# Third batch's first DFT moved off the first block's buffers and banks, with ScalarE's work for that block in another order

## The chip, the cores and the metric

The kernel runs on one core of a Trainium2 chip. Its time is the device time of one execution in microseconds (us); lower is better. The core has five instruction queues: TensorE (PE in the profile; PEld is its weight load), VectorE (DVE), ScalarE (ACT), GpSimd (POOL) and SyncE (SP, which here only issues transfers). Each queue runs its instructions in the order in which they stand.

## What is computed

```python
def reference(x, filt_r, filt_i, w_gate, w_noise, noise, w1, w2):
    # x (8, 2496, 256): Fourier filter along the sequence of each batch
    X = np.fft.rfft(x, axis=1)
    y = np.fft.irfft(X * (filt_r + 1j * filt_i)[None], n=2496, axis=1)
    # 19968 tokens of 256 features, 8 experts of width 1024, two experts a token
    t = y.reshape(19968, 256)
    logits = t @ w_gate + np.log1p(np.exp(t @ w_noise)) * noise
    top2, top2_w = two_best_and_their_softmax(logits)
    out = 0
    for e in range(8):
        for k in range(2):
            mask = top2[:, k] == e
            out[mask] += top2_w[mask, k, None] * (np.maximum(t[mask] @ w1[e], 0) @ w2[e])
    return out
```

All values are float32. The products of the expert part are made of three products of rounded halves each (`_mm3`: high by high, high by low, low by high).

## The kernel before

The work has two streams. The first filters one batch after the other by a transform of 39 x 64 points, works out the gate, and writes which token goes to which expert into a list. The second, the mixture of experts, takes the tokens of one expert in blocks of 512 from that list: it gathers their rows, multiplies with `w1`, applies relu, multiplies with `w2`, and adds the rows to the output. Batches 0 and 1 are filtered before the first block (the *early* part); the other batches are filtered beside the blocks.

The steps of the filter that matter here, with the lines of the profile and the names of their tiles:

- `s1`, the first DFT of a batch: 11 products of two groups (L319, bank `q1`). Each needs one load `x` (L305). ScalarE copies the result to a tile `c` (`c1`, L362), and SP writes it to a table `fd` in DRAM (L363), from which later steps read (`fx`, L370). In the early part the third batch (batch 2, products 22 to 32) has this step run too, two products in each time slot from slot 26.
- `t3` and `i2`, the inverse transform of a half batch `n` (n = 2 and 3 are the two halves of batch 1): six times a transposition (L494), a copy by ScalarE to `tf` (L499), a product (L516, bank `q6`), and a copy by ScalarE to `yt` (L526; for odd n also L529), which SP writes to `y` (L531). Transposition and product take turns on two banks, so a product waits until ScalarE has copied the one before it.
- the gate of a batch: products `lg` (L475 to L477), then a chain of small steps. ScalarE takes an exponential (L733), loads a table (`ACT_TABLE_LOAD`) and takes a logarithm (L736); VectorE works down to the counts `rs` (L737 to L772), with a second exponential by ScalarE (L766) between. TensorE makes prefix sums `rk` (L788 to L790), VectorE turns them into positions and `new` (L798 to L854), TensorE makes `sl` (L859, L860), VectorE makes `sval` (L861 to L880), TensorE makes `st` (L884), and VectorE makes the table `tab`. Then the list is built: 11 groups of products `ra` of masks `oc` (L921 to L926), a transposition (L933), and a scatter by GpSimd to `lst` (L945).
- `zero_out` writes zeros to the output rows of a batch in four parts (L293, 702 KB, the last 468 KB).

The steps of a block: SP reads its list (`lt`, L963), GpSimd gathers four tiles of rows (L999), ScalarE reorders them (L1049, `x32`), TensorE transposes (`xps`, L1057), ScalarE and VectorE split them into `mxh` and `mxl` (L1060, L1061). `w1` and `w2` come in four parts each through four slots of the tile `stage` and are split by ScalarE and VectorE (`wsplit`, L1107, L1108; w1 as `w1h` and `w1l`, w2 as `w`). Then eight times 6 products into a bank `hps` (L123 to L125), relu by ScalarE (L1150, `hh`) and the rest by VectorE (L1151, `hl`), and four times 24 products into `yps`. The first two blocks have rows of batch 0.

Three things set the order. `fft_stream` writes the early steps into numbered slots (`plan`), and `pin` ties each such instruction to the one pinned before it on its engine. Within that, a scheduler places instructions by its own estimate of times. And tiles of one tag share a few buffers in turn (`bufs`): the next user of a buffer waits for the last reader of the one before. PSUM banks go the same way, by tables:

```python
EARLY = {"q1": "hps", "q2": "hps", "q5": "yps", "q6": "yps", "u1": "xps"}
BANKS = {"hps": 2, "yps": 2, "xps": 1, "fps": 3}
MOVES = {..., 14: {"q3": "yps", "q4": "yps", "q5": "hps", "q6": "hps"}, 26: {"q4": "fps", "q5": "yps", "q6": "yps"}}
def ps(self, nm):
    tag = self.banks.get(nm, "fps") if self.early else "fps"
```

So a name that no table holds (`lg`, `rk`, `sl`, `st`, `ra`) takes one of the three banks `fps`, in the order in which the code asks. In slot 26 the code asks for `lg`, then for the third batch's products 22 and 23, then for `rk`, `sl` and `st` (all within slot 26, in `gating_more`), then in slot 27 for products 24 and 25. In the kernel before, the third batch's products take the two banks `hps`, its `x` the eight buffers `hh` and its `c` the eight buffers `hl`: the buffers and banks that the first block's eight results need.

Of the kernel before, what the change touches and what calls it, by code (L numbers as in the profile page):

```python
# [10 lines left out]
F32 = mybir.dt.float32  # L11
# [3 lines left out]
U16 = mybir.dt.uint16  # L15
AF = mybir.ActivationFunctionType
# [123 lines left out]

MOVES = {0: {"q3": "yps"}, 12: {"q3": "fps"}, 14: {"q3": "yps", "q4": "yps", "q5": "hps", "q6": "hps"}, 26: {"q4": "fps", "q5": "yps", "q6": "yps"}}


class Moe:
# [156 lines left out]
    def s1l(self, bt, g0):  # L301

        x = self.P.tile([128, 512], F32, name="x", **((dict(tag="w1l", bufs=4) if bt == 0 and g0 >= 16 else dict(tag="hh", bufs=8)) if self.early else dict(bufs=2)))

        self.lastx = self.nc.sync.dma_start(x, self.io["x"][bt, :, g0 * D:(g0 + 2) * D])  # L305
        x = x[:RP]
        self.xx[bt, g0] = x
        return self.lastx
# [50 lines left out]
    def s1e(self, bt, g0, q):  # L359
        nc, P, early = self.nc, self.P, self.early  # L360
        c = P.tile([120, 2, D], F32, name="c1", **(dict(tag="hl", bufs=8) if early else dict(bufs=1)))
        nc.scalar.copy(c, q.rearrange("p (g d) -> p g d", g=2))  # L362
        self.lastx = nc.sync.dma_start(self.Fd[bt][3 * g0:3 * g0 + 6].rearrange("(g q) k d -> (q k) g d", g=2), c)  # L363
# [144 lines left out]
    def i2(self, n, g0):  # L508
        nc, P, h = self.nc, self.P, n % 2
        Dh, Dl = self.cD  # L510
        th, tl = self.t3t.pop((n, g0))
        k = min(4, NG - g0)
        m = 128 * k
        p = self.ps("q6")
        if tl is None:
            nc.tensor.matmul(p[:RP, :m], self.rD, th[:120, :m], start=True, stop=True)  # L516
        else:
            nc.tensor.matmul(p[:RP, :m], Dh, th[:120, :m], start=True, stop=False)  # L518
            nc.tensor.matmul(p[:RP, :m], Dh, tl[:120, :m], start=False, stop=False)  # L519
            nc.tensor.matmul(p[:RP, :m], Dl, th[:120, :m], start=False, stop=True)  # L520
        w = 128 + E * h
        if n == 0:
            yt = P.tile([RP, 4, 128], F32, name="yt", tag=("mxl0", "mxh1", "mxl1")[g0 // 4 % 3], bufs=1)
        else:
            yt = P.tile([RP, 4, 128 + E], F32, name="yt", bufs=2)
        nc.scalar.copy(yt.bitcast(U16)[:, :k, :256].rearrange("p g (two d) -> p g two d", two=2),  # L526
                       p.bitcast(U16)[:RP, :2 * m].rearrange("p (g d two) -> p g two d", g=k, two=2))
        if h:
            nc.scalar.copy(yt[:, :k, 128:], self.dense[:, g0:g0 + k])  # L529
        y = self.y[BLK + n // 2 * ROWS:BLK + (n // 2 + 1) * ROWS].rearrange("(p g) d -> p g d", p=RP)  # L530
        nc.sync.dma_start(y[:, g0:g0 + k, h * 128:h * 128 + w], yt.bitcast(I32)[:, :k, :w])  # L531

    def fft_stream(self):
# [5 lines left out]
        N = 2 * NB  # L539
        self.fx, self.Fd = {}, {}  # L540
        todo = [(bt, g) for bt in range(NB) for g in range(0, NG, 2)]
# [10 lines left out]
        def s1(j):  # L552
            if self.early:
                self.s1(*todo[j])
                ahead(min(j + 9, 11 * (j // 11) + 11))
            else:
                ahead(j + 2)
                self.s1(*todo[j])
# [44 lines left out]
        at(8, self.setup2)  # L603
        at(20, ahead, 30)

# [17 lines left out]
        for i in range(4):  # L623
            at(18 + i, self.zero_out, 0, i)
            at(24 + i, self.zero_out, 1, i)

# [345 lines left out]
    def front(self, ent, fill=None):  # L972
# [6 lines left out]
        w1st = self.load_w(re, "w1", nt)  # L979
        w1 = [self.wsplit(w1st[q], "w1", q) for q in range(4)]  # L980
        w2st = self.load_w(re, "w2", nt)
# [51 lines left out]
    def turn(self, ent):  # L1033
# [8 lines left out]
        for kc in range(2):  # L1042
# [5 lines left out]
            else:  # L1048
                nc.scalar.copy(xu.rearrange("p (t d two) -> p t d two", t=nt, two=2),  # L1049
                               self.picked(ent).bitcast(U16)[:, :, 256 * kc:256 * kc + 256].rearrange("p t (two d) -> p t d two", two=2))  # L1050
            q.append(x)
        for kc in range(2):
            x = q[kc]
# [65 lines left out]
    def expert(self, parts, may, fill=None):  # L1119

        nc, P = self.nc, self.P
        self.parts, self.ahead, self.standing, self.early_l = parts, [], False, None
        self.fetch(lambda: True)
        cur = None
        while self.ahead:
# [10 lines left out]
            if not self.ahead or self.ahead[0][3] or sum(len(a[2][0]) for a in self.ahead) < 4:  # L1136
                self.fetch(may)
            third = ("xps", 1) if self.by_dma(ent) else ("yps", 2)
            hh = []
            for f in range(8):  # L1140
# [8 lines left out]
                l = P.tile([128, 512], R32, name="hl", bufs=8)[:, :w]  # L1149
                nc.scalar.activation(h, p, AF.Relu)  # L1150
                v = nc.vector.scalar_tensor_tensor(l, p, 0.0, f32v(h), op0=ALU.max, op1=ALU.subtract)  # L1151
                if f == 4:
                    self.early_l = v
                hh.append((h, l))
                if f % 2 and i == 0:
                    w2.append(self.wsplit(w2st[f // 2], "w2", f // 2))
                yield
            late = not self.ahead
            if late:
# [142 lines left out]
```

## Time and profile before

| | |
|---|---|
| time, three executions | 2263.53 us median, 2259.55 to 2263.73 |
| the profiled execution | 2255.39 us, span of its instructions 2253.5 us |
| TensorE busy | 2199.0 us (98% of the span), mean granted clock 0.992 |
| VectorE, ScalarE, GpSimd busy | 1621.7, 1240.4 and 955.1 us |
| first product of the first block | 166.11 us after the start |

A row of a timeline reads: start, duration, engine, line, operation, out<-in, shapes, count, and in brackets the idle time of the engine ahead of it and what ended it. Rows of equal instructions that follow each other are merged. A row of a window table gives, for each engine, the busy time within that stretch, then the granted TensorE clock (1.00 is full), the busy share of the DMA engines, and GB/s.

### The profile page before, as it was taken

Reading aid. Unit: us, or ns where it says so; the run is one execution under the profiler, and the core shown is the slowest. Engines: PE = TensorE matmul, PEld = TensorE weight load, DVE = VectorE, ACT = ScalarE, POOL = GpSimd, SP = SyncE. Lnnn points to the kernel's source line nnn. Section 1 sums busy time; section 2 is a strip of 40 time slices with the busy share of each in tenths; the row PEclk is TensorE's granted clock in tenths of the full one; section 3 lists DMA queues with packets and bytes.
Section 4 is the critical chain, followed back from the end, with each engine's and each line's share of the span. In section 5 each row is a group of like instructions: output and inputs, shape, how many; then the busy total and the mean of one; then the engine's idle time right before and its main releaser. Section 6 shows DMA issues by size and latency. Waiting matters only on the chain.

```text
span 2253.5 us, 39355 instructions
## 1 busy us (share of the span) xinstructions
PE 2199.0 (98%) x12599; PEld 1842.5 (82%) x12599; DVE 1621.7 (72%) x3494; ACT 1240.4 (55%) x2433; POOL 955.1 (42%) x822
## 2 busy tenths in 40 slices
PE   8779999999999999999999999999999999999998
PEld 5448888888888888888888888888888888889997
DVE  4858679779877987697668866795555555667886
ACT  6765655656566456445544455444444434557876
POOL 4013345335333444354344533355454544455442
PEclk9989999999999999999999999999999999999999
DMA  8678777887998677667665657565655555878774
GB/s 237 187 235 206 183 185 179 206 195 172 196 216 191 136 160 180 144 146 172 147 142 121 142 126 167 103 132 111 128 115 119 117 123 128 177 163 241 220 210 130
DMA packets 437610, 371.10 MB, mean 165 GB/s; under 512 B 187819, under 2 KB 347539, under 8 KB 437395
## 3 DMA queue, kind: packets, MB, share of 16 engines
q1 hardware_dynamic: 376083, 284.11, 46.8%
q0 software_dynamic: 61312, 84.40, 23.2%
q8 instruction: 101, 1.65, 0.3%
q14 instruction: 114, 0.93, 0.1%
HBM read 227.73 MB, written 105.25 MB: 148 GB/s over the span
## 4 chain that ended last, share of the span: by engine, by line
PE 89%; DVE 3%; ACT 3%; DMA 3%; issue 2%; SPq 1%; POOL 0%; DVEq 0%; POOLq 0%; ACTq 0%
PE yps L1177 20%; PE hps L123 13%; PE hps L124 12%; PE hps L125 12%; PE yps L1178 10%; PE yps L125 3%; PE yps L123 3%; PE yps L124 2%; PE q L430 2%; PE q L494 1%; DMA stage<-w 1%; PE u L441 1%; PE q L518 1%; PE q L319 1%; PE q L519 1%
## 5 line engine op out<-in xcount | busy, mean ns | idle before, releaser
L1185 POOL DMA_INDIRECT out<-stage,ids x316 | 540.9, 1712 | 444.3 <-DVE stage L1184 216.9
L1177 PE MATMUL yps<-w,hh 128*128 128x512 f32 x1952 | 688.1, 398 | 0.4 <-DVE stage L1184 0.4
L999 POOL DMA_INDIRECT stage<-y,ids x316 | 331.1, 1048 | 543.1 <-DMA xt<-stage 392.8
L124 PE MATMUL hps<-mxl,w1h 128*128 128x512 f32 (+2 forms) x1424 | 530.7, 374 | 0.3 <-DVE mxl L1061 0.3
L125 PE MATMUL hps<-mxh,w1l 128*128 128x512 f32 (+2 forms) x1424 | 525.1, 370 | 0.0
L1178 PE MATMUL yps<-w,hl 128*128 128x256 f32 x1952 | 521.9, 281 | 0.0
L123 PE MATMUL hps<-mxh,w1h 128*128 128x512 f32 (+2 forms) x1424 | 517.8, 376 | 1.1 <-DVE hl L1151 0.9
L1151 DVE SCALAR_TENSOR_TENSOR hl<-hps,hh 128x512 fp32r<-128x512 f32 (+2 forms) x712 | 433.3, 624 | 96.6 <-ACT hh L1150 93.4
L1150 ACT ACTIVATE hh<-hps 128x512 fp32r<-128x512 f32 (+2 forms) x712 | 381.3, 554 | 195.5 <-PE hps L125 179.3
L1177 PEld LDWEIGHTS yps<-w,hh 128*128 128x128 f32 x1952 | 357.1, 188 | 77.4 <-issue 1.9
L1178 PEld LDWEIGHTS yps<-w,hl 128*128 128x128 f32 x1952 | 366.8, 188 | 27.3 <-issue 1.8
L1182 ACT ACTIVATE stage<-yps,gt 128x256 f32<-128x256 f32 x316 | 142.5, 478 | 366.2 <-PE yps L1178 212.7
L125 PEld LDWEIGHTS hps<-mxh,w1l 128*128 128x128 f32 x1424 | 268.3, 188 | 48.0
L124 PEld LDWEIGHTS hps<-mxl,w1h 128*128 128x128 f32 x1424 | 268.6, 189 | 40.9 <-DVE mxl L1061 0.7
L123 PEld LDWEIGHTS hps<-mxh,w1h 128*128 128x128 f32 x1424 | 263.8, 188 | 43.1 <-DVE hl L1151 5.7
L1184 DVE SCALAR_TENSOR_TENSOR stage<-yps,gt,stage 128x256 f32<-128x256 f32 x244 | 112.2, 479 | 215.2 <-ACT stage L1182 214.7
L1107 ACT CAST w1h<-stage 128x512 fp32r<-128x512 f32 x192 | 119.2, 621 | 114.3 <-DMA stage<-w 55.0
L1108 DVE TENSOR_TENSOR w1l<-stage,w1h 128x512 fp32r<-128x512 f32 x192 | 130.9, 686 | 54.5 <-ACT w1h L1107 54.0
L123 PE MATMUL yps<-w,hh 128*128 128x256 f32 x576 | 164.0, 288 | 2.8 <-ACT hh L1150 2.7
L124 PE MATMUL yps<-w,hh 128*128 128x256 f32 x576 | 160.9, 285 | 0.0
L125 PE MATMUL yps<-w,hl 128*128 128x256 f32 x576 | 159.3, 286 | 0.0
L1108 DVE TENSOR_TENSOR w<-stage,w 128x512 fp32r<-128x512 f32 x228 | 152.4, 683 | 7.5 <-ACT w L1107 7.3
(226 smaller groups left out, 3048.1 us busy)
## 6 DMA issues: line engine op xcount, KB each, us to landing
stage<-w SPq DMA_DIRECT2D x420, 256.0 KB
x<-x SPq DMA_DIRECT2D x88, 256.0 KB
fd<-c SPq DMA_DIRECT2D x77, 240.0 KB
wb<-w SPq DMA_DIRECT2D x18, 1024.0 KB
fx<-fd SPq DMA_DIRECT2D x140, 128.0 KB
out<-z SPq DMA_DIRECT2D x24, 702.0 KB
y<-yt SPq DMA_DIRECT2D x40, 248.6 KB
y<-yt SPq DMA_DIRECT2D x40, 234.0 KB
```

The costliest lines, as they stand in the source:

```text
L123: nc.tensor.matmul(o, lh, rh, start=start, stop=False)
L124: nc.tensor.matmul(o, lh, rl, start=False, stop=False)
L125: nc.tensor.matmul(o, ll, rh, start=False, stop=stop)
L999: self.pin(lambda: nc.gpsimd.indirect_dma_start(out=x.bitcast(I32), out_offset=None, in_=self.y[:BLK + ready * ROWS], in_offset=bass.Indir ...
L1107: nc.scalar.copy(h, sv)
L1108: nc.vector.tensor_sub(l, sv, f32v(h))
L1150: nc.scalar.activation(h, p, AF.Relu)
L1151: v = nc.vector.scalar_tensor_tensor(l, p, 0.0, f32v(h), op0=ALU.max, op1=ALU.subtract)
L1177: nc.tensor.matmul(bank, h, hl, start=(f == 0), stop=False)
L1178: nc.tensor.matmul(p, l, hl[:, 0], start=False, stop=(f == 7))
L1182: nc.scalar.activation(o, p, AF.Copy, scale=gate[:, t])
L1185: a = nc.gpsimd.indirect_dma_start(out=self.io["out"][:BLK + ready * ROWS], out_offset=bass.IndirectOffsetOnAxis(ap=ids[:, t:t + 1], axis= ...
```

## The change

Five parts, all about the early part and the first blocks.

1. From slot 26 on the third batch's first DFT takes the banks `fps` in place of `hps`; the first block's third bank is `hps` in place of `yps`.
2. Its `x` goes to buffers `tl`, `fx` and `x` (two each that are free) in place of `hh`, its `c` to two buffers `a`, two places in the output slots of `stage`, and one of its own, in place of `hl`. Loads run 7 products ahead in place of 9, and 6 of them are asked for ahead of slot 26 in place of 8.
3. The eight writes of zeros go from slots 18 to 21 and 24 to 27 to slots 15 to 19, and one to 24.
4. ScalarE's work for the first block is held back by added order: the split of the first half of `w1` comes after the second `yt` of half batch 2, that of the second half after the third, and `x32` after the fifth.
5. Within the first block, the split of each part of `w2` comes after the relu of its time (before, it could come at any time), and the second block's `x32` after the fifth relu.

```diff
-MOVES = {..., 26: {"q4": "fps", "q5": "yps", "q6": "yps"}}
+MOVES = {..., 26: {"q1": "fps", "q4": "fps", "q5": "yps", "q6": "yps"}}
...
     def s1l(self, bt, g0):
-        x = self.P.tile([128, 512], F32, name="x", **((dict(tag="w1l", bufs=4) if bt == 0 and g0 >= 16 else dict(tag="hh", bufs=8)) if self.early else dict(bufs=2)))
+        if not self.early:
+            home = dict(bufs=2)
+        elif bt == 2:
+            home = (dict(tag="tl", bufs=3) if g0 < 4 else dict(tag="fx", bufs=2) if g0 % 8 >= 4 else dict(bufs=2))
+        else:
+            home = dict(tag="w1l", bufs=4) if bt == 0 and g0 >= 16 else dict(tag="hh", bufs=8)
+        x = self.P.tile([128, 512], F32, name="x", **home)
...
     def s1e(self, bt, g0, q):
-        c = P.tile([120, 2, D], F32, name="c1", **(dict(tag="hl", bufs=8) if early else dict(bufs=1)))
+        i = g0 // 2 % 5 if early and bt == 2 else None
+        if i in (2, 3):
+            at = 2048 + 4 * YW + 512 * (i - 2)
+            c = self.stage[:120, at:at + 512].rearrange("p (g d) -> p g d", g=2)
+        else:
+            home = dict(tag="hl", bufs=8) if early and i is None else dict(tag="a", bufs=2) if i in (0, 1) else dict(bufs=1)
+            c = P.tile([120, 2, D], F32, name="c1", **home)
...
     def i2(self, n, g0):
-        nc.scalar.copy(yt..., p...)
+        e = nc.scalar.copy(yt..., p...)
+        if n == 2:
+            self.yev.append(e)
...
-                ahead(min(j + 9, 11 * (j // 11) + 11))
+                ahead(min(j + (9 if j < 22 else 7), 11 * (j // 11) + 11))
...
-        at(20, ahead, 30)
+        at(20, ahead, 28)
...
-            at(18 + i, self.zero_out, 0, i)
-            at(24 + i, self.zero_out, 1, i)
+            at((15, 16, 17, 17)[i], self.zero_out, 0, i)
+            at((18, 18, 19, 24)[i], self.zero_out, 1, i)
...
     def front(self, ent, fill=None):
-        w1 = [self.wsplit(w1st[q], "w1", q) for q in range(4)]
+        for q in range(4):
+            with self.after(self.yev[1 + q // 2] if self.yev else None):
+                w1.append(self.wsplit(w1st[q], "w1", q))
...
     def turn(self, ent):
+                with self.after(self.yev[4] if self.yev else self.early_h):
+                    nc.scalar.copy(xu..., self.picked(ent)...)
...
     def expert(self, parts, may, fill=None):
-            third = ("xps", 1) if self.by_dma(ent) else ("yps", 2)
+            third = ("xps", 1) if self.by_dma(ent) else ("hps", 2) if self.first else ("yps", 2)
...
-                    w2.append(self.wsplit(w2st[f // 2], "w2", f // 2))
+                    with self.after(r if self.first else None):
+                        w2.append(self.wsplit(w2st[f // 2], "w2", f // 2))
```

What it does to the queues is not to be read from the diff, since the scheduler orders anew. Three places follow. A row names the line, the operation and out<-in; the changed kernel's lines are 6 higher from L305 on, 12 from L362, 14 from L531 and L730, and 19 or 20 in the block's code (so L802 is the old L788). `q` with a number is one bank's use.

First place: TensorE at the third batch's products 24 and 25. Before, from the fourth product `i2` of half batch 2 (`q_1424`) to the gate's `rk`:

```order
L516 MATMUL q_1424<-tf,cm 117x512
L319 MATMUL q_1429<-x,cm 120x512
L319 MATMUL q_1436<-x,cm 120x512
L494 MATMUL q_1442<-ident,G 120x128 x2
L1057 MATMUL xps<-ident,stage 128x128 x4
L516 MATMUL q_1447<-tf,cm 117x512
L494 MATMUL q_1452<-ident,G 120x128 x4
L516 MATMUL q_1459<-tf,cm 117x256
L319 MATMUL q_1464<-x,cm 120x512
L319 MATMUL q_1469<-x,cm 120x512
L1057 MATMUL xps<-ident,stage 128x128 x3
L788 MATMUL rk<-rs,small 117x8
```

The changed kernel, on TensorE from the same fourth `i2` (`q_1421`):

```order
L528 MATMUL q_1421<-tf,cm 117x512
L802 MATMUL rk<-rs,small 117x8
L803 MATMUL rk<-rs,small 128x8
L804 MATMUL rk<-small,rs 8x1
L873 MATMUL sl<-new,small 8x1
L874 MATMUL sl<-new,small 8x1
L898 MATMUL st<-sval,small 1x64
L325 MATMUL q_1426<-x,cm 120x512
L325 MATMUL q_1432<-x,cm 120x512
L506 MATMUL q_1438<-ident,G 120x128 x2
L528 MATMUL q_1443<-tf,cm 117x512
```

All three steps of the gate, `rk`, `sl` and `st`, have moved ahead of products 24 and 25, with nothing between them; before, `sl` and `st` stood 11 and 19 rows behind `rk`. The banks of products 24, 25 and 26 are the ones that `rk`, `sl` and `st` had.

Second place: ScalarE from the first `yt` of half batch 2 on. Before:

```order
L526 COPY yt<-q_1288 117x4x256
L1107 CAST w1h<-stage 128x512
L499 COPY tf<-q_1293 120x512
L1107 CAST w1h<-stage 128x512
L733 ACTIVATE rank_94<-lg 117x176
L1107 CAST w1h<-stage 128x512
L526 COPY yt<-q_1300 117x4x256
L1107 CAST w1h<-stage 128x512
L362 COPY c_1308<-q_1306 120x512
L736 ACT_TABLE_LOAD
L736 ACTIVATE gl<-rank_95 117x176
```

The changed kernel, on ScalarE from the same `yt` to the fourth one:

```order
L538 COPY yt<-q_1286 117x4x256
L511 COPY tf<-q_1291 120x512
L747 ACTIVATE rank_94<-lg 117x176
L750 ACT_TABLE_LOAD
L750 ACTIVATE gl<-rank_95 117x176
L538 COPY yt<-q_1298 117x4x256
L1126 CAST w1h<-stage 128x512 x2
L374 COPY c_1306<-q_1304 120x512
L374 COPY c_1313<-q_1311 120x512
L511 COPY tf<-q_1402 120x512
L538 COPY yt<-q_1409 117x4x256
L1126 CAST w1h<-stage 128x512 x2
```

The gate's two exponentials and the table load have moved ahead of the second `yt` and of all splits of `w1`.

Third place: TensorE at the first block's first products. Before they stand behind the last of the third batch's DFT:

```order
L516 MATMUL q_1551<-tf,cm 117x512
L516 MATMUL q_1557<-tf,cm 117x256
L319 MATMUL q_1563<-x,cm 120x512
L123 MATMUL hps<-mxh_1756,w1h 128x512
L124 MATMUL hps<-mxl_1757,w1h 128x512
```

The changed kernel, on TensorE from the second half of the seventh `i2` on:

```order
L528 MATMUL q_1479<-tf,cm 117x512
L506 MATMUL q_1485<-ident,G 120x128 x4
L123 MATMUL hps<-mxh_1752,w1h 128x512 x2
L1076 MATMUL xps<-ident,stage 128x128 x4
L124 MATMUL hps<-mxl_1753,w1h 128x512
L125 MATMUL hps<-mxh_1752,w1l 128x512
L124 MATMUL hps<-mxl_1753,w1h 128x512
L125 MATMUL hps<-mxh_1752,w1l 128x512
L528 MATMUL q_1492<-tf,cm 117x512
```

The first block's products now stand among the last five products `i2` (`q_1492` is the eighth of twelve) and the last five of the third batch's DFT.

More of the change, by code (lines that the diff above doesn't have):

```diff
@@ L139 @@
 BANKS = {"hps": 2, "yps": 2, "xps": 1, "fps": 3}
-MOVES = {0: {"q3": "yps"}, 12: {"q3": "fps"}, 14: {"q3": "yps", "q4": "yps", "q5": "hps", "q6": "hps"}, 26: {"q4": "fps", "q5": "yps", "q6": "yps"}}
+MOVES = {0: {"q3": "yps"}, 12: {"q3": "fps"}, 14: {"q3": "yps", "q4": "yps", "q5": "hps", "q6": "hps"}, 26: {"q1": "fps", "q4": "fps", "q5": "yps", "q6": "yps"}}
 class Moe:
@@ L525, in i2 @@
             yt = P.tile([RP, 4, 128 + E], F32, name="yt", bufs=2)
-        nc.scalar.copy(yt.bitcast(U16)[:, :k, :256].rearrange("p g (two d) -> p g two d", two=2),
+        e = nc.scalar.copy(yt.bitcast(U16)[:, :k, :256].rearrange("p g (two d) -> p g two d", two=2),
                        p.bitcast(U16)[:RP, :2 * m].rearrange("p (g d two) -> p g two d", g=k, two=2))
+        if n == 2:
+            self.yev.append(e)
         if h:
@@ L539, in fft_stream @@
         N = 2 * NB
-        self.fx, self.Fd = {}, {}
+        self.fx, self.Fd, self.yev = {}, {}, []
         todo = [(bt, g) for bt in range(NB) for g in range(0, NG, 2)]
@@ L979, in front @@
         w1st = self.load_w(re, "w1", nt)
-        w1 = [self.wsplit(w1st[q], "w1", q) for q in range(4)]
+        w1 = []
+        for q in range(4):
+            with self.after(self.yev[1 + q // 2] if self.yev else None):
+                w1.append(self.wsplit(w1st[q], "w1", q))
         w2st = self.load_w(re, "w2", nt)
@@ L1048, in turn @@
             else:
-                nc.scalar.copy(xu.rearrange("p (t d two) -> p t d two", t=nt, two=2),
-                               self.picked(ent).bitcast(U16)[:, :, 256 * kc:256 * kc + 256].rearrange("p t (two d) -> p t d two", two=2))
+                with self.after(self.yev[4] if self.yev else self.early_h):
+                    nc.scalar.copy(xu.rearrange("p (t d two) -> p t d two", t=nt, two=2),
+                                   self.picked(ent).bitcast(U16)[:, :, 256 * kc:256 * kc + 256].rearrange("p t (two d) -> p t d two", two=2))
             q.append(x)
+        self.yev = []
         for kc in range(2):
@@ L1122, in expert @@
         self.parts, self.ahead, self.standing, self.early_l = parts, [], False, None
+        self.early_h, self.first = None, True
         self.fetch(lambda: True)
@@ L1149, in expert @@
                 l = P.tile([128, 512], R32, name="hl", bufs=8)[:, :w]
-                nc.scalar.activation(h, p, AF.Relu)
+                r = nc.scalar.activation(h, p, AF.Relu)
                 v = nc.vector.scalar_tensor_tensor(l, p, 0.0, f32v(h), op0=ALU.max, op1=ALU.subtract)
                 if f == 4:
-                    self.early_l = v
+                    self.early_l, self.early_h = v, r if self.first else None
                 hh.append((h, l))
                 if f % 2 and i == 0:
-                    w2.append(self.wsplit(w2st[f // 2], "w2", f // 2))
+                    with self.after(r if self.first else None):
+                        w2.append(self.wsplit(w2st[f // 2], "w2", f // 2))
                 yield
+            self.first = False
             late = not self.ahead
```

## The prediction

> **What bounds the kernel now.** I read the page's slices first, then windows around the change, then the waits of TensorE in them, then the timelines of the engines that TensorE waits for.
>
> ```profile
> span 2253.5 us, 39355 instructions
> PE   8779999999999999999999999999999999999998
> PEclk9989999999999999999999999999999999999999
> ```
>
> A slice is 56 us. TensorE is full but for the first 170 us and the very end, and the only slice at a low clock is the third (113 to 169 us): the change's place. In windows (per engine busy time, then clock, DMA share, GB/s; TensorE is the first number behind the window's length):
>
> ```profile
> 0.00:118.00 118.00, 96.28 (x548) 61.87 (x548) 73.28 (x221) 74.96 (x134) 24.08 (x28) 0.96 0.74 216
> 118.00:139.30 21.30, 13.96 (x48) 8.12 (x46) 10.86 (x29) 15.32 (x26) 8.08 (x10) 0.74 0.74 222
> 139.30:166.10 26.80, 21.38 (x91) 11.06 (x90) 19.54 (x101) 19.88 (x34) 2.44 (x4) 0.94 0.78 240
> 166.10:202.00 35.90, 35.90 (x230) 30.59 (x228) 26.75 (x61) 19.37 (x38) 9.63 (x9) 1.00 0.63 166
> 202.00:223.00 21.00, 17.22 (x97) 14.76 (x97) 18.67 (x30) 12.68 (x25) 9.94 (x11) 0.95 1.19 262
> ```
>
> TensorE is idle 7.3 us in 118 to 139.3 (21.30 less 13.96), 5.4 us in 139.3 to 166.1, nothing in 166 to 202, 3.8 us in 202 to 223, where the second block enters. So the most that the change can fill is 7.3 + 5.4 + 3.8 = 16.5 us, and a little of lost clock. TensorE's waits in 118 to 168 (total, times, longest), and its rows there:
>
> ```profile
> PE q L516 <- ACT yt L526: 7.8, 6, 3.3
> PE q L494 <- ACT tf L499: 4.9, 2, 2.5
> ```
>
> ```profile
> 123.72 1.12 PE L516 MATMUL q<-tf,cm 120*117 120x512 f32 x2 [0.18 <-ACT yt L526]
> ...
> 130.28 1.12 PE L516 MATMUL q<-tf,cm 120*117 120x512 f32 x2 [3.27 <-ACT yt L526]
> 133.91 1.11 PE L494 MATMUL q<-ident,G 128*120 128x128 f32 x4 [2.51 <-ACT tf L499]
> ...
> 137.46 2.06 PE L516 MATMUL q<-tf,cm 120*117 120x512 f32 x2 [1.37 <-ACT yt L526]
> 139.31 3.42 PE L319 MATMUL q<-x,cm 117*120 117x512 f32 x4
> ...
> 148.59 1.88 PE L319 MATMUL q<-x,cm 117*120 117x512 f32 x4
> ...
> 150.64 0.28 PE L788 MATMUL rk<-rs,small 117*117 117x8 f32 x2
> ...
> 163.45 0.27 PE L884 MATMUL st<-sval,small 8*1 8x64 f32 x2
> ...
> 166.11 0.80 PE L123 MATMUL hps<-mxh,w1h 128*128 128x512 f32 x1
> ```
>
> All of it is ScalarE, and ScalarE is late because its queue holds splits of `w1` that wait for the weights, and a table load, ahead of `yt` and `tf`:
>
> ```profile
> 122.66 1.01 ACT L526 COPY yt<-q 117x1024 uint16<-117x1024 uint16 x1 [0.42 <-PE q L516]
> 125.20 0.62 ACT L1107 CAST w1h<-stage 128x512 fp32r<-128x512 f32 x1 [1.53 <-DMA stage<-w]
> 125.73 0.58 ACT L499 COPY tf<-q 120x512 f32<-120x512 f32 x1
> ...
> 126.73 0.32 ACT L733 ACTIVATE rank<-lg 117x176 f32<-117x176 f32 x1
> 128.70 0.62 ACT L1107 CAST w1h<-stage 128x512 fp32r<-128x512 f32 x1 [1.65 <-DMA stage<-w]
> ...
> 131.25 1.28 ACT L736 ACT_TABLE_LOAD   x1
> 132.55 0.35 ACT L736 ACTIVATE gl<-rank 117x176 f32<-117x176 f32 x1
> ...
> 143.22 0.62 ACT L1107 CAST w<-stage 128x512 fp32r<-128x512 f32 x1 [2.66 <-DMA stage<-w]
> ```
>
> The gate's chain, which VectorE works off from `gl` on, is long. Its rows, up to `rs`, then behind `rk` to `new`, and behind `sl` to the last `sval`:
>
> ```profile
> 132.93 0.25 DVE L737 TENSOR_SCALAR rank<-rank 117x176 f32<-117x176 f32 x1 [1.46 <-ACT gl L736]
> ...
> 139.66 0.69 DVE L1061 TENSOR_TENSOR mxl<-xps,mxh 128x512 fp32r<-128x512 f32 x1
> ...
> 143.88 0.69 DVE L1108 TENSOR_TENSOR w<-stage,w 128x512 fp32r<-128x512 f32 x1 [2.54 <-ACT w L1107]
> ...
> 148.71 0.46 DVE L772 TENSOR_REDUCE rs<-rank 117x8 f32<-117x176 f32 x1
> ...
> 151.30 0.16 DVE L798 SCALAR_TENSOR_TENSOR rw<-mm,rk 128x8 int32<-128x8 f32 x1 [0.49 <-PE rk L790]
> ...
> 154.97 0.13 DVE L854 CAST new<-ci 8x1 f32<-8x1 int32 x1
> ...
> 157.72 0.64 DVE L922 TENSOR_TENSOR oc<-oc,half 117x224 f16<-117x224 f16 x3
> 158.35 0.14 DVE L861 TENSOR_TENSOR st<-nblk,sl 8x1 f32<-8x1 f32 x1
> ...
> 159.86 0.22 DVE L880 TENSOR_SCALAR sval<-sge,small 8x32 f32<-8x32 f32 x1
> ```
>
> From `gl` to `rs` took 16.2 us (132.93 to 149.17), `rk` to `new` 3.8 us, `sl` to the last `sval` 1.7 us. Nothing on TensorE waited for them, since products stood between.
>
> **The change, part by part.** *Banks.* `rk`, `sl` and `st` take the three banks `fps` in turn, and after the change the third batch's products 24, 25 and 26 ask for those three banks next. TensorE's order shows what follows: all three gate steps stand right behind the fourth product `i2`, with nothing between, ahead of products 24 and 25. TensorE passes nothing in its queue, so each leg of the gate's chain becomes idle time, less what TensorE is late anyway. When is the chain done?
>
> `gl` comes earlier. The first `yt` ends at 123.67; then `tf` 0.58, `rank` 0.32, table 1.28, `gl` 0.35: 126.2, against 132.90 before. VectorE then needs the 16.2 us less the 2.54 us wait for a `w` split (which part 5 puts behind the block's relu), so 13.7 with four foreign rows of 0.69, as now four `w1l` splits stand in the chain in place of `w` and `mxl`. That gives 139.9. But the last two of these splits need ScalarE's casts behind the third `yt`, and ScalarE comes to them late: the second `yt` ends at 127.3, two casts (1.2), two `c` and a `tf` (1.7) at 130.2, the third `i2` at 131.3, its `yt` at 132.3, a cast at 132.9. VectorE would have been there at about 131.5, so it waits 1 to 1.5 us. `rs` ends near 141 (bounds 138.5, if VectorE's foreign rows find gaps, and 142.4, the whole 16.2 us).
>
> TensorE reaches `rk` at about 135: another cast and a `tf` (1.2) behind 132.9, then the fourth `i2` (1.12). So it waits 6 us. `rk` itself takes 0.66 (150.64 to the start of `rw`), then 3.8 us to `new`, some 0.4 for `sl`, then 1.7 us and, since mask builds `oc` and casts to `lo` stand between there, up to 2.8 more, then `st` 0.3. Sum: 141 + 0.7 + 3.8 + 0.4 + 4.5 + 0.3 = 150.7. Product 24 began at 139.31 before, which is +11.4 us, bounds +8 (`rs` at 138.5, half of the `oc` rows between) and +13 (`rs` at 142.4). The work done by then differs little: `rk`, `sl` and `st`, 0.9 us, are ahead, one `xps` group, 0.5 us, is behind: -0.4.
>
> *Clock.* Behind the stall TensorE is slow for a while: the rows at 137.46 (2.06 for what takes 1.12 at 123.72) and 139.31 (3.42 for what takes 1.88 at 148.59) lose 0.9 + 1.5 us, 2.5 us. Before had that loss too, 1.5 of it behind 139.3; now it lies wholly behind product 24: +1. The Trainium skill, "TensorE: Matmul & The Clock Gate", Part 1: The HAM clock gate, says that after an idle window of some 3.4 us the clock is halved until about 3.4 us of sustained work have passed. By that alone the loss would be 1.7 us in place of 2.5, and the time 0.8 us lower; the trace's clock of 0.74 in 118 to 139.3 agrees in kind.
>
> *The first block's products among the rounds* (third order place). Before, 139.31 to 166.11 holds the 5.4 us idle. Now the first block's eight groups of six products can fill waits of the last five rounds: 48 products, at least 7.5 us (the window 166.1 to 202 holds 230 products, many of them shorter, in 35.90 us: 0.156 each). But ScalarE is stopped too, since the `c` of product 24 stands next in its queue, and keeps behind it what it had before (19.88 us of this window) plus the relus of the first groups, beside TensorE's 21.38 + 7.5 = 28.9. Each waits for the other now and then, and product 24, now late, frees the `x` buffer of load 28 late, with SP's next `y` write queued behind that load: I allow 1 to 8 us of idle for all of it, and take 4.3, nearer to the 5.4 of before than to none, since these waits are the same ones: -1.1.
>
> *Zero writes and loads.* Eight writes, 5.15 MB, leave the stretch from 118 on for 80 to 107 us, among `fx` loads and `y` writes. Whatever they delay there reaches `yt` of batch 1; ±1 us, taken as 0, since the DMA share of 0 to 118 (0.74) equals that of 118 to 139.3 (0.74). Six loads asked ahead in place of eight cost SP nothing that TensorE sees: TensorE is stalled when products 24 on need them.
>
> *ScalarE's order.* The waits of 1.53, 1.65 and 2.66 us vanish from ScalarE. The first two are what the early `gl` above uses; the third freed VectorE (the 2.54). The `x32` copies that stood ahead of product 24 now stand behind it on ScalarE, and are part of the idle allowed there.
>
> *The second block.* Its list comes out of `ra`; the transposition and the scatter, the first rows of its gathered tiles on VectorE, and TensorE's wait:
>
> ```profile
> 183.28 0.27 PE L933 MATMUL ra<-ident,rx 128*56 128x128 f32 x1
> ```
>
> ```profile
> 189.29 1.49 POOL L945 DMA_INDIRECT lst<-ro,row  x1 [0.31 <-issue]
> ```
>
> ```profile
> 213.54 0.94 DVE L1047 COPY stage<-xt 128x1024 uint16<-128x1024 uint16 x1
> ```
>
> ```profile
> 220.62 0.39 PE L123 MATMUL yps<-w,hh 128*128 128x256 f32 x1 [2.67 <-ACT hh L1150]
> ```
>
> From the list's transposition to the block's input passed 30 us (183.28 to 213.54). In the changed order about 27 us of products stand between, against 34 before, so this wait (3.8 us idle in 202 to 223) is not filled: 0, bounds -2 and +7. What is late next is this list.
>
> **Sum:** +11.4 - 0.4 + 1.0 - 1.1 + 0 + 0 = +10.9; I take +10, since of the 2.8 us of `oc` and casts a part can run while VectorE waits for `sl`. The profiled execution (2255.39 us, span 2253.5) would take 2265.4; it lies 8.1 us below the median of the runs, 2263.53, so against that median I forecast 2273.5. The bounds of the terms (8 to 13 for the stall, -4.4 to +2.6 for the later idle, and half of -2 to +7 at the second block) reach from 2267 to 2281 for this case.
>
> **The rivals.**
> - *Faster: the rounds run without the stall.* If `gl` is earlier by 6.7 us and VectorE, free of foreign work, has `rs` by 135, `rk` costs little, and the first block's products and ScalarE's shorter queue fill the idle of 118 to 166 (12.7 us, less some 3 that stays). It decides if product 24 begins before about 141. The time: -6 to -10, near 2255. For it: the waits on `yt` and `tf` are nearly all the idle there is, and both come from ScalarE's queue. Against it: of the 13.7 us from `gl` to `rs` all but the four splits are the gate's own rows, and `rk` to `sval` adds 5.5 us that no edit shortens.
> - *No net change: the stall is paid and given back.* After it ScalarE has caught up (its splits and fourth `yt` are done while TensorE stands), so that the rounds behind run without waits, and 5.4 + 1.5 (clock) + 3.8 us = 10.7 of later idle go. It decides if TensorE's idle from product 24 to the second block's entry is under 2 us. Time: 2262 to 2267. For it: 166.1 to 202 shows that TensorE runs full when it has the block's products to choose from. Against it: those products stand in fixed order, not by readiness.
> - *Worse: the second block waits.* If the list, 12 us of products later in TensorE's order, starts its 30 us to the block's input later than the work before that block covers, 5 to 7 us are added: +15 to +20, near 2281.
> - That nothing moves is excluded by the order.
>
> **How the numbers follow.** The forecast (+10) has 0.55, faster 0.20, no net change 0.17, the second block's wait 0.08. 0.2%, 4.5 us, is about what a measurement can tell from no change here. Faster by more: 0.21 (the first rival and a rest); within: 0.18; slower: 0.61 (forecast and worse, less 0.02). The range 2256 to 2283 leaves out the lower half of the first rival (0.10) and the upper part of the worst (0.05). The likeliest case's own is 2267 to 2281.
>
> **What would show it.** TensorE's waits would name VectorE ahead of `rk` (about 6 us), `sl` and `st` (about 4 each), product 24 would begin near 150 in the changed kernel, `gl` near 126, `rs` near 141, and the clock would be low from about 137 to 154. Behind that, TensorE's idle up to 166 would be small, and the list's scatter some 10 us later than 189.29. I am wrong if product 24 begins before 145, if `rk`, `sl` and `st` show no waits, or if the stretch from product 24 to 223 holds less than 2 us idle.

## The result, and the profile after

The changed kernel took 2286.59 us (median of four runs, 2279.77 to 2292.71), the kernel before 2263.58 (2259.55 to 2263.73): a ratio of 1.0105, interval 1.0077 to 1.0132. Run again beside the last experiments, it came out at 1.0080 (1.0066 to 1.0094). The forecast was 2273.5 with a range of 2256 to 2283: the sign was right, the size about half, and the time lies above the range.

First the windows of the changed kernel, cut at product 24 (151.73), with the whole of 118 to 260; then the kernel before, from its product 24 (139.31) on and again the whole. Columns as in the prediction: length, busy time of TensorE first, then clock, DMA share, GB/s.

```profile
118.00:151.73 33.73, 13.63 (x61) 7.04 (x61) 23.64 (x111) 13.75 (x23) 6.62 (x8) 0.66 0.35 102
151.73:200.00 48.27, 41.90 (x183) 27.41 (x183) 16.17 (x42) 30.03 (x53) 4.02 (x5) 0.85 0.57 165
200.00:260.00 60.00, 53.45 (x343) 46.45 (x341) 43.33 (x79) 31.23 (x58) 28.65 (x26) 0.97 0.86 204
118.00:260.00 142.00, 108.98 (x583) 80.90 (x583) 83.14 (x231) 75.01 (x134) 39.29 (x39) 0.86 0.64 167
```

```profile
139.31:188.00 48.69, 43.27 (x232) 29.39 (x231) 36.54 (x145) 32.91 (x59) 3.10 (x5) 0.97 0.68 206
118.00:260.00 142.00, 125.47 (x696) 96.43 (x694) 100.86 (x257) 88.44 (x161) 44.26 (x45) 0.94 0.79 209
```

Between 118 and 260 TensorE is idle 33.0 us (142 less 108.98), against 16.5 before. Part of the busy time is lost too, where the clock is low. The clock of a row is a mean over time, idle time included, so it can't simply be multiplied with the busy time. Cut where the clock changes, every stretch has 0.50 or 1.00. These are the ones at 0.50, in the changed kernel and then in the kernel before (the busy time of TensorE is again the first number behind the length):

```profile
128.80:151.73 22.93, 4.82 (x18) 2.39 (x18) 17.23 (x91) 5.09 (x8) 1.34 (x3) 0.50 0.32 101
151.73:156.11 4.38, 4.38 (x8) 2.09 (x8) 0.52 (x4) 1.16 (x3) 0.00 (x0) 0.50 0.25 72
159.52:166.35 6.83, 5.18 (x10) 2.76 (x11) 0.00 (x0) 5.12 (x7) 1.57 (x2) 0.50 0.34 87
173.17:176.59 3.42, 3.42 (x5) 1.30 (x4) 0.69 (x1) 2.31 (x5) 0.19 (x1) 0.50 0.00 0
248.27:251.68 3.41, 3.24 (x9) 2.67 (x10) 2.93 (x5) 2.74 (x6) 2.37 (x3) 0.50 1.34 276
```

```profile
118.00:121.91 3.91, 3.91 (x18) 3.29 (x16) 1.96 (x10) 1.65 (x4) 1.02 (x1) 0.50 0.30 63
132.15:139.31 7.16, 4.03 (x11) 2.21 (x12) 5.67 (x13) 7.15 (x12) 2.46 (x3) 0.50 0.93 276
139.31:142.39 3.08, 3.08 (x5) 1.20 (x4) 1.96 (x6) 1.12 (x2) 2.25 (x3) 0.50 0.99 314
220.90:224.31 3.41, 3.41 (x18) 3.41 (x18) 3.38 (x7) 2.19 (x5) 1.88 (x2) 0.50 0.95 264
```

Half of the busy time in them is lost, which is an estimate: 10.5 us (21.04 / 2) against 7.2 (14.43 / 2). Idle and lost time together are 16.5 + 3.3 = 19.8 us more than before, most of the 23.0 between the medians. The loss is complete soon after: GpSimd's 600th gather or scatter from the end begins at 309.27 against 287.67, its 60th from the end at 2065.96 against 2044.33, both 21.6 us later.

TensorE's waits of the changed kernel in 118 to 200 (total, times, longest):

```profile
PE q L528 <- ACT yt L538: 10.9, 4, 4.3
PE rk L802 <- DVE rs L786: 6.0, 1, 6.0
PE sl L873 <- DVE new L868: 4.0, 1, 4.0
PE st L898 <- DVE sval L894: 3.7, 1, 3.7
```

The gate's three waits, 13.7 us, are new; the waits for `yt` have not gone, they have grown (7.8 before). Their rows on TensorE:

```profile
134.31 2.06 PE L528 MATMUL q<-tf,cm 120*117 120x512 f32 x2 [4.32 <-ACT yt L538]
142.32 0.56 PE L802 MATMUL rk<-rs,small 117*117 117x8 f32 x2 [5.95 <-DVE rs L786]
...
147.46 0.20 PE L873 MATMUL sl<-new,small 8*8 8x1 f32 x2 [4.02 <-DVE new L868]
...
151.44 0.37 PE L898 MATMUL st<-sval,small 8*1 8x64 f32 x2 [3.73 <-DVE sval L894]
151.73 3.77 PE L325 MATMUL q<-x,cm 117*120 117x512 f32 x4
...
161.17 1.20 PE L528 MATMUL q<-tf,cm 120*117 120x256 f32 x2 [3.79 <-ACT yt L538]
162.17 3.62 PE L325 MATMUL q<-x,cm 117*120 117x512 f32 x4
...
172.70 1.63 PE L528 MATMUL q<-tf,cm 120*117 120x512 f32 x2 [2.58 <-ACT yt L538]
```

Product 24 begins at 151.73. What follows is no recovery: two more waits for `yt`, and the next pair of products, behind the first of them, takes 3.62 us again in place of 1.88. ScalarE shows what `yt` waits for, and SyncE's queue why:

```profile
133.25 1.01 ACT L538 COPY yt<-q 117x1024 uint16<-117x1024 uint16 x1 [4.41 <-DMA y<-yt]
...
160.10 1.01 ACT L538 COPY yt<-q 117x1024 uint16<-117x1024 uint16 x1 [3.71 <-DMA y<-yt]
...
171.64 1.01 ACT L538 COPY yt<-q 117x1024 uint16<-117x1024 uint16 x1 [3.97 <-DMA y<-yt]
```

```profile
125.47 0.85 SPq L545 DMA_DIRECT2D y<-yt  x2
...
153.82 0.35 SPq L311 DMA_DIRECT2D x<-x  x1
...
155.53 0.35 SPq L311 DMA_DIRECT2D x<-x  x1
155.93 0.94 SPq L545 DMA_DIRECT2D y<-yt  x2
...
164.11 0.36 SPq L311 DMA_DIRECT2D x<-x  x1
...
165.82 0.36 SPq L311 DMA_DIRECT2D x<-x  x1
166.27 0.87 SPq L545 DMA_DIRECT2D y<-yt  x2
```

The first of these waits, which ends at 133.25, has no load `x` to blame: the writes ahead of it went out at 125.47. A variant that runs level with the kernel before (`x` in `hh`, below) has this wait too, 3.81 us long. Why the write took so long isn't shown.

The other two are SyncE's. The `yt` made at 133.25 and 136.40 are ready 18 us before SyncE writes them out at 155.93. For most of that time SyncE stands at a read of the gate's table (`tabi`, a copy of `tab`), which it needs for a block's list. Then two loads `x` stand ahead of the write. Each takes a buffer that a product frees, so each goes out just behind a product of the pair (151.73), and these loads are what ends last. With the next pair the loads alone repeat it (162.17, then 164.11 to 166.27). SyncE's waits in 118 to 200 put numbers on both:

```profile
SPq L311 <- PE q L325: 16.4, 5, 8.3
SPq L975 <- DVE tabi L906: 14.8, 1, 14.8
```

The kernel before had neither row. The second one is the gate's early place once more: with the gate on `hps` (below) it is gone as well.

The profile pair differs by more than the medians (2286.7 against 2253.5 us of span). Beside the 21.6 us above, the part from GpSimd's 60th gather or scatter from the end takes 220.7 us in the changed kernel's profile and 209.2 in that of before. A repeat of the changed kernel has 222.7 there, but so has, on that chip, a variant that runs as fast as before (the last row of the table below, 222.8). The order of the executed instructions is the same in that part; as far as these profiles show, it is not the change.

### The profile page after: what moved, and what is told of

Its sections match the earlier page's. It is cut to its first block, busy times and chain, and to the rows that moved or that the text cites. A ratio compares the mean times of both kernels' runs of the same rounds, so it can differ in the third digit from the quotient of the medians.

```text
span 2286.7 us, 39342 instructions
## 1 busy us (share of the span) xinstructions
PE 2208.0 (97%) x12599; PEld 1843.5 (81%) x12599; DVE 1621.9 (71%) x3494; ACT 1238.7 (54%) x2433; POOL 946.8 (41%) x822
## 4 chain that ended last, share of the span: by engine, by line
PE 85%; DVE 1%; DMA 1%; issue 1%; ACT 0%; SPq 0%; POOL 0%; POOLq 0%; DVEq 0%; ACTq 0%
PE yps L1199 19%; PE hps L123 13%; PE hps L125 12%; PE hps L124 12%; PE yps L1200 10%; PE yps L123 3%; PE yps L125 3%; PE yps L124 3%; PE q L442 2%; PE q L506 1%; PE u L453 1%; PE q L530 1%; PE q L531 1%; PE q L532 1%; DMA stage<-w 1%
## 5 line engine op out<-in xcount | busy, mean ns | idle before, releaser
L1207 POOL DMA_INDIRECT out<-stage,ids x316 | 533.9, 1690 | 406.9 <-DVE stage L1206 211.4
```

The source lines that it names most:

```text
L1207: a = nc.gpsimd.indirect_dma_start(out=self.io["out"][:BLK + ready * ROWS], out_offset=bass.IndirectOffsetOnAxis(ap=ids[:, t:t + 1], axis= ...
```

## The experiments

Times of one group of runs were taken on one chip and compared with runs of the kernel before on it: 2251.2 us for the first group, 2250.9 for the second, 2267.7 for the third. Only ratios compare across groups. The times in the expectations of the first group were reckoned on the 2263.5 us above and have to be read as differences to that. The changed kernel itself was not run on the chips of the first two groups, and its two ratios differ by 0.0025; so what a single part is worth there is known to about 0.003. Last two columns: idle TensorE and mean clock (over time, idle included) in 118 to 260 of each profile, from its window row.

| kernel | ratio to before (interval) | idle, us | clock |
|---|---|---|---|
| before | 1 | 16.5 | 0.94 |
| changed | 1.0105 (1.0077-1.0132), 1.0080 (1.0066-1.0094) | 33.0 | 0.86 |
| old banks | 1.0044 (1.0031-1.0058) | 20.5 | 0.90 |
| gate on hps | 1.0032 (1.0020-1.0044) | 23.0 | 0.93 |
| old buffers | 1.0068 (1.0055-1.0081) | 29.0 | 0.90 |
| old zeros | 1.0123 (1.0108-1.0137) | 34.6 | 0.86 |
| gate on hps, old buffers | 0.9996 (0.9984-1.0007) | 13.7 | 0.96 |
| gate on hps, 5 ahead | 1.0002 (0.9993-1.0011) | 15.3 | 0.95 |
| gate on hps, x in hh | 0.9988 (0.9979-0.9996) | 16.4 | 0.94 |
| old ScalarE order | 1.0145 (1.0128-1.0163) | 35.9 | 0.87 |
| 5 ahead alone | 1.0043 (1.0028-1.0057) | 24.0 | 0.89 |
| idle products (their time counts as busy) | 1.0089 (1.0073-1.0105) | 23.9 | 0.86 |
| gate on hps, x in hh, later w1 | 0.9997 (0.9987-1.0008) | 15.4 | 0.96 |

**Old banks.** `"q1": "fps"` out of slot 26, the first block's third bank `yps` again; the rest as changed.

> The changed kernel with its part on the banks taken back: the third batch's first DFT keeps the two banks hps, the first block's third bank is yps. In its order, rk stands 9 rows later on TensorE (behind products 24 to 27), sl 11 rows behind rk, st 8 behind sl. Theory A (the loss of 23 us is mainly the gate's chain rk, sl, st standing in TensorE's way, because it shares the banks fps with products 24 to 26; 12.4 us of stall and some 5 us of low clock behind it in the profile of the changed kernel): the stall goes, product 24 begins below 142 us, time 2263 to 2271. Theory B (the loss is mainly SyncE's queue: loads x into few buffers, standing ahead of the y writes, which make yt wait 3.7 to 4.4 us three times): those waits stay, time 2276 to 2286, although rk no longer stalls.

2262.0 us, ratio 1.0044: about half of the loss goes with the banks (0.0061 of 0.0105, or 0.0036 of 0.0080), and 11 us stay. That lies between theory A (up to +7.5 us) and theory B (from +12.5), so neither holds alone: in this profile TensorE waits for no gate step, and 13.4 us for `yt`.

**Gate on hps.** The banks stay as changed, and only the gate's steps take others:

```diff
-26: {"q1": "fps", "q4": "fps", ...}
+26: {"q1": "fps", "rk": "hps", "sl": "hps", "st": "hps", "q4": "fps", ...}
```

> The changed kernel with one addition to the table of banks: from slot 26 on rk, sl and st take the two banks hps. The third batch's first DFT stays on fps. Its order on TensorE up to st is that of the kernel with the old banks. Theory A (the gate's chain in TensorE's way): like the kernel with the old banks, within 5 us of it, 2260 to 2271; product 24 begins below 142. If the first block's products or banks were at fault in themselves, and not the gate's place, this one stays above 2276. Theory B (SyncE's x loads): 2276 to 2286.

2258.6 us, 1.0032, within 4 us of the kernel above: what cost was the place of the gate's steps in TensorE's queue, not the move of `q1` nor the block's bank. Most of the waits left are those behind SyncE:

```profile
145.86 0.36 SPq L311 DMA_DIRECT2D x<-x  x1
...
147.57 0.33 SPq L311 DMA_DIRECT2D x<-x  x1
147.99 0.88 SPq L545 DMA_DIRECT2D y<-yt  x2
```

```profile
153.81 1.01 ACT L538 COPY yt<-q 117x1024 uint16<-117x1024 uint16 x1 [3.45 <-DMA y<-yt]
```

**Old buffers.** `x` in `hh`, `c1` in `hl`, 9 loads ahead; the banks as changed.

> The changed kernel with its part on the buffers taken back: x in the eight buffers hh, c1 in the eight buffers hl, loads 9 products ahead, 8 of them ahead of slot 26. The order on TensorE still has rk, sl and st ahead of product 24. Theory A: the stall stays (product 24 begins near 151), only the waits of yt behind the y writes shrink, 3 to 5 us of 23: 2279 to 2286. Theory B: the waits were the loss: 2264 to 2272.

2266.1 us, 1.0068: +14.9 us, between theory B (up to +8.5) and theory A (from +15.5), and nearer to A. The gate's waits are as in the changed kernel. Theory A, which I held, had put the buffers at 3 to 5 us; they are worth 8 by the changed kernel's 1.0105 and 3 by its 1.0080.

```profile
PE rk L790 <- DVE rs L774: 5.9, 1, 5.9
...
PE sl L861 <- DVE new L856: 4.0, 1, 4.0
PE st L886 <- DVE sval L882: 3.7, 1, 3.7
```

**Old zeros.** The eight writes back in slots 18 to 21 and 24 to 27.

> The changed kernel with the writes of zeros back in slots 18 to 21 and 24 to 27; nothing else. TensorE's order around the gate is that of the changed kernel. Theory A and B: both put the cost elsewhere, so within 5 us of the changed kernel, 2280 to 2292. Theory C (the earlier writes delay the inverse transform of batch 1, or the late ones were cheap): below 2278.

1.0123, no better than the changed kernel; the earlier zeros cost nothing that can be measured.

**Both causes taken away.** Gate on hps and old buffers together:

> The changed kernel with rk, sl and st on the two banks hps from slot 26 on, and with the old buffers for x and c1 (x in hh, c1 in hl, loads 9 ahead). Kept of the change: the third batch's first DFT on fps, the writes of zeros, ScalarE's order. Two-cause theory (gate's chain in TensorE's way, and x loads ahead of y writes in SyncE's queue; taken alone, the first brought 1.0105 to 1.0032, the second 1.0105 to 1.0068, together more than the whole loss): ratio to the kernel before 0.998 to 1.002, no wait of yt for a y write above 1 us. A third cause (ScalarE's order, or the zeros): 1.003 or more.

0.9996: nothing is left of the loss. The gate's banks alone leave 1.0032, the buffers alone 1.0068, and the three intervals don't touch: each is a cause, and together they are the whole. From 1.0105 the two shares, 0.0073 and 0.0037, add up to the 0.0109 of both; from 1.0080 they would not (0.0048 and 0.0012 against 0.0084), so how they add stays open.

**Gate on hps, 5 loads ahead.** One number on top of the kernel with the gate on hps:

```diff
-ahead(min(j + (9 if j < 22 else 7), ...))
+ahead(min(j + (9 if j < 22 else 5), ...))
```

> The kernel with the gate on hps (1.0032), and one number changed: the third batch's loads x are asked 5 products ahead in place of 7, so that a load stands in SyncE's queue behind the product that frees its buffer and not four products earlier. Buffers as in the changed kernel. Theory (what costs is the place of the x loads in SyncE's queue, not the number of buffers): the three waits of yt for y writes (10.9 us in all there) fall under 4 us, and the ratio to 0.999 to 1.001. Rival (too few buffers, whatever the place): the ratio stays at 1.003, or the products wait for x instead.

1.0002, against 1.0032 without it. The buffers are as few as in the changed kernel, so it is the place of the loads in SyncE's queue that cost, and not the number of buffers. ScalarE's waits for `y` writes in 115 to 200 are 3.6 us, against 10.9.

**Gate on hps, x in hh.** Only `x` goes back to its old buffers; `c1` stays in its new ones.

> The kernel with the gate on hps, and x back in the buffers hh with 9 loads ahead; c1 stays in its new places. Theory (x loads in SyncE's queue): like the kernel with both old buffers, within 0.001 of it, 0.998 to 1.002. Rival (c1 in few buffers: ScalarE waits until a copy c is written out before it can make the next): 1.002 to 1.004, with waits of ScalarE's c for writes fd.

0.9988, slightly under the kernel with both old buffers: `c1` in few buffers costs nothing. Its ratio is the lowest of all; 0.12% is less than the 0.2% that counts here, so I call it level with the kernel before.

**Old ScalarE order.** Parts 4 and 5 taken back.

> The changed kernel without the added order on ScalarE (parts 4 and 5); banks, buffers and zeros as changed. In its order the first block's first products stand ahead of rk, sl, st on TensorE, and product 24 still behind them. Theory A (the chain rk to st still stands ahead of product 24): it stays above 1.008, product 24 begins no earlier than 148 us, since w1's splits again wait for weights ahead of the gate's logarithm. Rival (the added order is what costs): 1.006 or less.

1.0145: the added order is no cost, it saves 0.4 to 0.65% beside the other parts, by the two ratios of the changed kernel. Without it product 24 began at 172.84, behind products of the first block and all three gate steps.

**5 loads ahead alone.** The same one number, in the changed kernel itself:

> The changed kernel with the one number alone: the third batch's x asked 5 products ahead in place of 7. The gate's stall stays. Theory of two independent causes: with the gate on hps this number was worth 0.0030; the same here, 1.0065 to 1.0085, waits of yt for y writes under 5 us (12.8 in the changed kernel). Rival (behind the stall other waits take their place): 1.0095 or more.

1.0043, against 1.0080 for the changed kernel beside it: 0.0037, about the 0.0030 seen with the gate on hps. The ratio lies under the expected 1.0065 to 1.0085, which was reckoned from 1.0105. The gate's stall is untouched, and SyncE still waits 13.6 us for `tabi`, but the `y` writes now stand ahead of that read and go out at 132.83 and 135.99. The rest comes right:

```profile
150.28 3.77 PE L325 MATMUL q<-x,cm 117*120 117x512 f32 x4
...
157.70 1.88 PE L325 MATMUL q<-x,cm 117*120 117x512 f32 x4
```

```profile
150.28:200.00 49.72, 48.71 (x269) 35.33 (x269) 21.38 (x58) 33.76 (x61) 8.82 (x8) 0.94 0.67 189
```

The second pair of products is at full speed, and behind product 24 TensorE is idle 1.0 us in place of 6.4, at a clock of 0.94 in place of 0.85.

**Idle products in the stall.** 33 products that nobody reads, to keep TensorE busy while it waits for the gate:

```diff
+    def warm(self, t, n):
+        d = self.PS.tile([128, 512], F32, name="dm", tag="hps", bufs=2)
+        k, w = t.shape[0], t.shape[-1]
+        self.nc.tensor.matmul(d[:k, :w], self.tri[:k, :k], t, start=True, stop=True)
+        for _ in range(n):
+            self.nc.tensor.matmul(d[:RP, :RP], self.tri[:RP, :RP], self.tri[:RP, :RP], ...)
...
+            self.warm(c[0], 10)    # ahead of rk
+            self.warm(self.cnt, 8) # ahead of sl
+            self.warm(st, 12)      # ahead of st
```

> The changed kernel with 33 idle products added on TensorE into a bank hps that nobody reads: 11 ahead of rk (the first reads a step of the gate some 3 us ahead of rs), 9 ahead of sl, 13 ahead of st, in the time in which TensorE stood still. Everything else in the same order. Clock theory (the stall costs a second time, since products 24 and 25 and what follows run at a low clock: 3.77 us in place of 1.88, clock 0.86 in 118 to 260 against 0.94, about 7.7 us): the two products take about 1.9 us, and the ratio falls by 0.001 to 0.003. Rival (TensorE waits for ScalarE and SyncE there, so a faster clock only waits longer): no change within 0.001, or slower.

```profile
138.10 0.56 PE L804 MATMUL rk<-rs,small 117*117 117x8 f32 x2
...
146.31 4.69 PE L862 MATMUL dm<-small 117*117 117x117 f32 x24
151.13 1.98 PE L325 MATMUL q<-x,cm 117*120 117x512 f32 x4
160.56 3.62 PE L325 MATMUL q<-x,cm 117*120 117x512 f32 x4
```

1.0089, no gain. The clock theory's first half holds: product 24's pair takes 1.98 us in place of 3.77. But the added products were too many: from `rk` to product 24 it now takes 13.0 us, against 9.4 in both profiles of the changed kernel, which eats the 1.8 us gained and more. And the next pair is slow again, behind its own wait for `yt`. The 7.7 us of the expectation multiply busy time with the mean clock; by the stretches at 0.50 it is 3.3 us, and 2.2 of the loss lie right behind the stall (half of 4.38). How much of these 2.2 us a well-measured filling would gain stays open.

**Later w1.** The kernel with `x` in `hh`, and the splits of `w1` one `yt` later each:

> The kernel with the gate on hps and x in hh (0.9988), and ScalarE's splits of w1 one yt later each (behind the third and the fourth yt of half batch 2, in place of the second and third). In that kernel ScalarE still waits 6.2 us for weights ahead of its yt and tf, and TensorE 9.3 us for those between 115 and 260. Theory (ScalarE's queue, with splits that wait for weights ahead of copies that TensorE needs, sets the pace there, as in the kernel before): faster than before, 0.996 to 0.998. Rival (the first block then waits for its w1, or the y writes set the pace): 0.9985 to 1.001.

0.9997, in the rival's range: nothing gained. ScalarE waits as long for weights as without this order (6.2 us) and longer for `y` writes (5.9 us against 3.8), so the run doesn't tell whether its waits for weights would set the pace if they were gone.

**The changed kernel again.**

> The changed kernel as it is, once more, beside the variants and for a second profile. In its first profile the last 260 us of the span held 15.6 us of idle TensorE, in before and in all eight variants 10.2 to 11.0, though the order of the executed part is the same there. If that was the chance of one execution, this profile has 10 to 11 us there; if it belongs to the change, again 15 or more. Ratio 1.008 to 1.013 either way.

1.0080, and 16.2 us of idle in the last 260 us, where the first profile had 15.6; the variant at 0.9997 has 15.5 there, on the same chip, so it does not look like the change's. The gate's three waits are the same here (6.0, 4.0 and 3.7 us), and product 24 begins at 149.50.

## Why the prediction was right in sign and half in size

- **The order and the stall: right.** `rk` waited 5.95 us (6 forecast), `sl` and `st` 4.02 and 3.73 (about 4 each), product 24 began at 151.73 (150.7): +12.4 us against +11.4, and +10.2 in the repeat. On the way two errors cancelled in part, which is luck. The logarithm ended at 125.03, ahead of the 126.2 forecast, but VectorE's wait for the third `w1` split was 4.90 us and not "1 to 1.5 us", since the third `yt` waited 4.41 us (2.54 in the repeat) for a `y` write that the forecast didn't have:

```profile
124.68 0.35 ACT L750 ACTIVATE gl<-rank 117x176 f32<-117x176 f32 x1
```

```profile
134.81 0.69 DVE L1127 TENSOR_TENSOR w1l<-stage,w1h 128x512 fp32r<-128x512 f32 x1 [4.90 <-ACT w1h L1126]
...
141.80 0.46 DVE L786 TENSOR_REDUCE rs<-rank 117x8 f32<-117x176 f32 x1
```

- **"I allow 1 to 8 us of idle for all of it, and take 4.3": the step that failed.** Its mechanism was named (a late product frees the buffer of load 28 late, with the `y` write behind that load), but taken once, as "the same" waits as before, and without any slow clock behind it. It comes back with every pair of products, 16.4 us of SyncE in five waits. Idle from product 24 to 200 was 6.4 us, 2.1 more than taken, and the low clock behind these waits cost 4.3 us more, for which the sum had nothing. SyncE's read of `tabi`, 14.8 us, was not in the prediction either.
- **The clock: +1.0 forecast, +4.9 measured.** In 151.73 to 200 half of 4.38, 5.18 and 3.42 us is lost, 6.5 us; in the like stretch of before half of 3.08, 1.5 us. The one slow spell that was charged, behind the gate's stall, cost 2.2 us, near the 2.5 forecast. The other 4.3 us lie behind the two waits for `yt`; 5 loads ahead, which takes these waits away, leaves only a spell of 5.54 us (half of it is 2.8 us). The Trainium skill, "TensorE: Matmul & The Clock Gate", "HAM oscillation — how this bites in real kernels", tells of idle gaps of more than about 3.4 us that come back and make TensorE slow again each time. The wait of 3.79 us, with the pair of 3.62 us behind it, agrees; the wait of 2.58 us is shorter than that, and the clock was 0.50 behind it too (173.17 to 176.59).
- **What the two are worth.** They are 2.1 + 3.9 = 6.0 us of the 13 that the forecast of +10 lacked. The one number that takes the waits away is worth 0.0037, or 8.4 us.
- **The second block: 0 forecast, +2.8.** In 200 to 260 TensorE idles 6.5 us, against 3.8 before, most of it in one wait for the next `w1` (4.1 us). The list's scatter came at 218.62, 29 us later than before and not "some 10". But the repeat idles only 4.6 us there, and the variants 2.4 to 7.2 (7.2 with the gate on hps), so the size is not sure, and I can't say which part brings it.

```profile
218.62 1.47 POOL L959 DMA_INDIRECT lst<-ro,row  x1 [5.45 <-DVE ro L956]
```

```profile
248.44 1.22 PE L123 MATMUL hps<-mxh,w1h 128*128 128x512 f32 x2 [4.10 <-ACT w1h L1126]
```

- **Sum by windows:** 12.4 for the stall, less 0.4 as forecast, +4.9 clock, +1.0 idle over the like stretch of before, +2.8 at the second block: 20.7, against 21.6 between the profiles at 310 us, 23 between the medians, and 18 by the repeat's ratio.
- **Two sums of the prediction don't come out.** The bounds of its terms reach 13 - 0.4 + 1 + 2.6 + 3.5 = +19.7, which is 2283 and not 2281. And +10 with 5 to 7 us at the second block is +15 to +17, not up to +20.
- **Zeros: right** (no measurable cost). **ScalarE's order: right** that it brings the logarithm forward; undone, the kernel is slower still.
- **The rivals.** "Paid and given back" needed later idle to vanish; it rose. "Faster" did not appear; where the gate was out of TensorE's way and the loads `x` no longer held up SyncE, the kernel came out level. "Worse" needed 5 to 7 us at the second block; the profiles have 2.8 and 0.8, so it is not what took the time above its 2281.

## What to carry to other kernels

When buffers or banks are shared anew, ask of each queue in order what now stands ahead of what: here a bank put a long chain of small steps ahead of products that didn't need it, and in another queue a read of that chain's result, and loads that wait for a buffer, went ahead of writes that were ready. A load into a buffer that a product frees is best asked for right behind that product: one number took the loss from 1.0032 to 1.0002 without a byte of memory. And price a wait that recurs by its count, with the slow clock behind each, not as one event.

## What had not been expected

- Two waits for `yt`, 3.79 and 2.58 us, cost another 4.3 us by the low clock behind them. In the kernel before, TensorE's wait of 2.42 us that ends at 146.66 cost nothing of the kind: there the clock is 1.00 all the way from 142.39 to 188.
- The gate's early place stopped SyncE too: it stood 14.8 us at a read of the gate's table, with `y` writes that were ready behind it.
- Keeping TensorE busy through the stall did restore the speed of the very next pair (1.98 us against 3.77), but not of the pair behind the next wait (3.62 us).
- With the same executed order at the end of the kernel, TensorE idled 10.2 to 11.0 us of the last 260 us in the profile of before and those of the first two groups, and 14.5 to 16.2 in all four of the third, on another chip; the first profile of the changed kernel has 15.6.
